# Sliding-window attention with a gated SwiGLU: edge blocks in smaller TensorE tiles, V for sixteen heads at a time

## Chip, cores and metric

The kernel runs on one core of one Trainium2 chip. The metric is the device time of one launch in microseconds (us). Three runs are timed, and a further execution is profiled.

## What is computed

```python
def reference(A_x, A_wqkv, A_wo, B_x, B_w1, B_w3, B_w2, gate_w):
    ...
        H = 32; Dh = D // H; W = 256
        qkv = (lambda x, *d: x.transpose(*d))((x @ wqkv).reshape(B, S, 3, H, Dh), 2, 0, 3, 1, 4)
        q, k, v = qkv[0], qkv[1], qkv[2]
        scores = jnp.einsum("bhqd,bhkd->bhqk", q, k) * (Dh ** -0.5)
        idx = jnp.arange(S)
        mask = (idx[:, None] - idx[None, :] >= 0) & (idx[:, None] - idx[None, :] < W)
        scores = jnp.where(mask[None, None], scores, -1e9)
        p = _softmax(scores, axis=-1)
        o = jnp.einsum("bhqk,bhkd->bhqd", p, v)
        return (lambda x, *d: x.transpose(*d))(o, 0, 2, 1, 3).reshape(B, S, D) @ wo
    ...
        gate = jnp.einsum("bsd,df->bsf", x, w1)
        up = jnp.einsum("bsd,df->bsf", x, w3)
        h = _silu(gate) * up
        out = jnp.einsum("bsf,fd->bsd", h, w2)
    ...
    g = _sigmoid((x * gate_w).sum(-1, keepdims=True))
    a = _A_ref(x, A_wqkv, A_wo)
    b = _B_ref(x, B_w1, B_w3, B_w2)
    return g * a + (1 - g) * b
```

B = 1, S = 2048, D = 512, F = 1376, all in bfloat16; both branches read A_x.

## The kernel before

**Attention.** The 32 heads of 16 channels go in four groups c of eight heads; a group's 128 channels fill the partitions, two heads (a = 0, 1) in each strip s of 32. `projections(c, tq)` computes K, Q and V for 512 tokens (L422 for K and Q, L499 for V). Since a strip holds two heads, K is kept once for each head with the other head's channels zeroed: `kz` and `k1`, made by masks at L465 and a copy at L462 (for c = 0 at L443, L448 and L453). `kz` has four blocks of 64 keys for each 128-key block t, so that two neighbouring ones hold the same 64 keys of both heads.

Keys come in 16 blocks t of 128. For queries P*t+64 to P*t+320 the whole block is scored: `main_batch(c, t)` makes eight products of 32 rows x 128 weight columns over 256 queries into the PSUM tile `su` (L560), ScalarE takes the exponential into `Em` (L564), and GpSimd cuts the two triangles (L569, L574). The 64 queries before (low) and after (high) see half the block: `edge_batch(c, h)` puts those of four blocks into one `su` (L610): 64 queries against a 128-column weight tile that holds 64 keys of both heads. After the exponential (L614) GpSimd cuts the low triangles (L627, two selects) and VectorE the high ones (L633, for the last batch L637 too, with the masks `medge` and `mlast`). The last key block's own 64 queries ride in the last edge batch.

`pv(c, w)` makes the value products for 512 queries (L700): for each head a of a strip one PSUM bank `ch`, four strips at once (128 rows x 17 columns, the 17th gives the softmax's sum). Mains and edges are mixed, first all of a = 0, then all of a = 1. The edges' values lie in two further parts of `vs` (LO, HI), in which the rows of the other head's keys are zero; L271 and L272 clear them, and GpSimd copies the halves (L517) after VectorE has evicted V (L512). Two 32x32-block transposes (L724), a reciprocal, a multiplication and a transpose back (L734) make the normalized output `OT`.

**The rest.** The SwiGLU runs beside it: w1 and w3 products into `ch` (L825), tanh on ScalarE (L835), two multiplications on VectorE (L839, L845), the w2 products (L875) and an eviction scaled by 1 - g (L880). 32 of the last 96 columns of F go another way, `tail_columns` (L785). The gate g comes as a 129th column of V's products in the first group (`wv0`, L521). `output` multiplies by wo (L905), adds, and stores.

**What sets the order.** A planner (`Plan.emit`) simulates the engines and buffers ahead of time and writes one fixed order for each engine. Every operation has a duration, dependencies, a due time (from the dictionary K) and the buffers it takes and frees: one `su`, four `ch` banks (shared by projections, V, value products, SwiGLU and output), nine `Em`, two `Ee`. For TensorE it knows forms: "full", "row" (scores) and "column" (value products), charges 0.117 us for a change, and `rank` moves due times so that operations of small forms stand together: earlier by `beside` when a small form is loaded, later by `apart` for "column" when "full" is.

Of the kernel before, what the change touches and what calls it, by code (L numbers as in the profile page):

```python
# [7 lines left out]
ALU = mybir.AluOpType  # L8
# [37 lines left out]
class Plan:  # L46
# [101 lines left out]
def kernel(  # L148
# [27 lines left out]
    NV = NT * 4  # L176
    LO, HI = NV, 2 * NV
    VW = DH + 1
    HALF = (0, 1, 2, 3, 4)
    SCALE = float(DH) ** -0.5  # L180
# [17 lines left out]
    wB = pp.tile([P, NDC, 2 * FB], BF16, name="wB")  # L198
# [8 lines left out]
    wv0 = pp.tile([P, NDC, P + 4], BF16, name="wv0")  # L207
# [8 lines left out]
    mlast = pp.tile([P, 2, KB], BF16, name="mlast")  # L216
    Em = [pp.tile([P, 4, 2, 256], BF16, name=f"Em_{i}") for i in range(9)]
    Ee = [pp.tile([P, 4, 4, 2, KB], BF16, name=f"Ee_{i}") for i in range(2)]
    kt = [pp.tile([P, 512], BF16, name=f"kt_{i}") for i in range(2)]
# [10 lines left out]
    K = {"T0": 6.663, "TA": 234.789, "TF0": -1.359, "TF1": 251.583, "PV": 0.213, "EDGE": -2.966, "HOLD": -4.301, "LEAD": 9.863, "QLEAD": -3.864, "V": 5.26, "O0": -0.819, "O1": 5.827, "O2": 6.852, "O3": 24.592, "FE": -3.084, "PE": -2.787, "VE": -3.291, "MK": 4.4, "UP": 2.598, "_km": 1.0, "_lo": 1.0, "LE": 4.467, "ADJ": 0.265, "SEP": 1.114, "BE": -2.825}  # L230
    plan = Plan({"su": 1, "ch": 4, "Em": len(Em), "Ee": len(Ee), "kt": 2, "tt": 2, "h1": 2,
# [4 lines left out]

    def half_of(base, a):
        return slice(0, KB) if (a == 1) == (base == LO) else slice(KB, P)
# [19 lines left out]
    def constants3():  # L258
        nc.gpsimd.memset(qT[:, S:S + KB], 0.0)
        for m in (medge, mlast):  # L260
            nc.gpsimd.memset(m[:], BIG)
        for m, k, sign, halves in ((medge, 0, 1, (0, KB)), (medge, 1, -1, (0, KB)),
                                   (mlast, 0, 1, (0, KB)), (mlast, 1, 1, (KB,))):
            for lo in halves:
                nc.gpsimd.affine_select(out=m[lo:lo + KB, k, :], in_=m[lo:lo + KB, k, :],
                                        pattern=[[sign, KB]], compare_op=ALU.is_ge, fill=0.0,
                                        base=0 if sign > 0 else -1, channel_multiplier=-sign)

    def constants4():
        nc.gpsimd.memset(hb[:], 0.0)  # L270
        nc.vector.memset(vs[:, LO:LO + NV, :], 0.0)  # L271
        nc.vector.memset(vs[:, HI:HI + NV, :], 0.0)  # L272
        nc.gpsimd.memset(vs[:, 0:NV, DH:2 * VW:VW], 1.0)
        for base in (LO, HI):
            for a in range(2):
                nc.gpsimd.memset(vs[half_of(base, a), base:base + NV, a * VW + DH], 1.0)

# [106 lines left out]
    def gw_out():  # L384
        nc.vector.tensor_copy(out=wv0[:, :, P:P + 1],
                              in_=ch[gjob.at["ch"]][:].bitcast(BF16)[:, 0:NDC].rearrange("p (c o) -> p c o", o=1))

    def wv0_copy():
        nc.vector.tensor_copy(out=wv0[:, :, 0:P], in_=wqkv_sb[:, :, 2 * D:2 * D + P])

    a = add("PE", 0.1, gw_turn, [gw_in], 9.407, take=[(gjob, "ch")])
    wv0_ready = [add("DVE", 0.15, gw_out, [a], 9.0, free=[(gjob, "ch")]),
                 add("DVE", 0.3, wv0_copy, [qkv_in[2]], 9.0)]
# [11 lines left out]
    def projections(c, tq):  # L405
# [3 lines left out]
        if c:  # L409
            war = [su_ops[(c - 1, t)] for t in range(4 * tq, 4 * tq + 4)]  # L410
            war.append(far_ops[(c - 1, tq)])
            vwar = [pv_ops[(c - 1, w)] for w in range(tq, min(NTC, tq + 2))]
            qwar = [su_ops[(c - 1, t)] for t in range(max(0, 4 * tq - 3), 4 * tq + 4)]
            qwar += [far_ops[(c - 1, h)] for h in range(max(0, tq - 1), tq + 1)]
        else:
            vwar, qwar = [], []
# [16 lines left out]
        kv0 = kz[:, 4 * tq:4 * tq + 4, 1:3, :]  # L433
        kv1 = kz[:, 4 * tq:4 * tq + 4, 0:4:3, :]

        k1v = k1[:, 4 * tq:4 * tq + 4, :, :]

        def by_half(src):
            return src.rearrange("p (k h t) -> p k h t", h=2, t=KB)
        a = project(kj, D, [qkv_in[0 if c < 2 else 3]], due, [(kj, "ch")])  # L440
        if c == 0:
            def kev_a():
                nc.vector.tensor_scalar_mul(  # L443
                    out=kv0, in0=by_half(ch[kj.at["ch"]][:]),
                    scalar1=rowsA[:, 0:1])

            def kev_b():
                nc.scalar.activation(  # L448
                    out=k1v, in_=by_half(ch[kj.at["ch"]][:]),
                    func=ACT.Copy, scale=rowsA[:, 1:2])  # L450
            b = add("DVE", 0.69, kev_a, [a], due, free=[(kj, "ch")])
            def kev_c():
                nc.gpsimd.tensor_copy(out=kv1, in_=k1v)  # L453
            m = add("ACT", 0.69, kev_b, [b], due, free=[(kj, "ch")])
            k_ready[(c, tq)] = [b, m]
            ke_ready[(c, tq)] = [add("POOL", 0.62, kev_c, [m], due)]
        else:
            def kev():
                nc.vector.tensor_copy(out=kt[kj.at["kt"]][:], in_=ch[kj.at["ch"]][:])

            def kcopy():
                (nc.vector if K["_km"] else nc.gpsimd).tensor_copy(out=kv1, in_=k1v)  # L462

            def kmask(h):
                (nc.vector if K["_km"] else nc.gpsimd).tensor_scalar_mul(  # L465
                    out=(kv0, kv1, k1v)[h], in0=by_half(kt[kj.at["kt"]][:]),
                    scalar1=rowsA[:, min(h, 1):min(h, 1) + 1])
            b = add("DVE", 0.69, kev, [a], due, take=[(kj, "kt")], free=[(kj, "ch")])
            k_ready[(c, tq)] = [add("DVE" if K["_km"] else "POOL", 0.3 if K["_km"] else 1.64, lambda h=h: kmask(h), [b] + war, due, free=[(kj, "kt")])
                                for h in (0, 2)]  # L470
            ke_ready[(c, tq)] = [add("DVE" if K["_km"] else "POOL", 0.3 if K["_km"] else 0.62, kcopy, k_ready[(c, tq)], due)]
# [12 lines left out]

        vdue = due + K["V"]
        res = []
        gates = []
        for m0, nm in ([(4 * tq, 2), (4 * tq + 2, 2)] if c == 0 else [(4 * tq, 4)]):
            vj = Job()
            w = P + 1 if c == 0 else P  # L490

            def vmm(lo, hi, vj=vj, m0=m0, w=w):
                pst = ch[vj.at["ch"]]
                for mm in range(lo, hi):
                    m = m0 + mm
                    for dc in range(NDC):
                        rhs = (wv0[:, dc, 0:w] if c == 0
                               else wqkv_sb[:, dc, 2 * D + c * P:2 * D + (c + 1) * P])
                        nc.tensor.matmul(pst[:, mm * w:(mm + 1) * w], lhsT=xT[:, dc, m * P:(m + 1) * P],  # L499
                                         rhs=rhs, start=(dc == 0), stop=(dc == NDC - 1))  # L500

            def v_of(rows, base, a, m0=m0, nm=nm):
                return vs[rows, base + 4 * m0:base + 4 * (m0 + nm), a * VW:a * VW + DH]

            def v_all(vj=vj, m0=m0, nm=nm, w=w):
# [463 lines left out]
```

## Time and profile before

| | |
|---|---|
| median of three timed runs | 240.3 us (240.14 to 240.38) |
| the profiled execution's own time | 240.56 us |
| its span in the profile | 238.8 us |
| granted TensorE clock | 1.00 |
| VectorE busy | 201.3 us (84%) |
| TensorE's waits for others, longest line | 1.7 us, two times (L700 for L839) |

The page lists for each engine its busy time in the span. PE is TensorE's matmuls and PEld its weight loads, which lie beside them; DVE is VectorE, ACT ScalarE, POOL GpSimd. Groups of instructions are named by line, engine, operation and tiles. In the timeline the first two columns are the start and the length of a run of equal instructions in us; matmuls overlap, so that a group's length is not the time that it takes from the next one: that is seen from start to start. A bracket at the end gives idle time of the engine before the instruction and what ended it.

### The profile page before, as it was taken

What the parts mean: (1) busy time and instruction counts of PE and PEld (TensorE: products, weight loads), DVE (VectorE), ACT (ScalarE), POOL (GpSimd) and SP (SyncE); (2) the same over time, 40 slices, a digit from 0 to 9 for tenths busy, and PEclk for the clock granted to TensorE, in tenths of its full rate; (3) what the DMA queues carried; (4) which work ended last, traced back from release to release, by engine and by line L of the source; (5) the groups of instructions that cost most, each with busy time, mean ns of one, the idle gap of its engine ahead of it and who ended that gap; (6) DMA issues with size and microseconds to landing.
All of it is one profiled execution on the core that took longest, in us unless ns stands there. A gap on an engine that the chain in (4) does not pass through costs nothing.

```text
span 238.8 us, 8528 instructions
## 1 busy us (share of the span) xinstructions
PE 231.3 (97%) x3738; PEld 118.8 (50%) x3738; DVE 201.3 (84%) x342; ACT 171.2 (72%) x141; POOL 159.6 (67%) x261
## 2 busy tenths in 40 slices
PE   8999999999999999999989899999999999999994
PEld 8554544546463543545454544545454545445442
DVE  5576998967699989996699999987899897969885
ACT  3389798876867898666858788776768989766510
POOL 7259967979857877587475777768494968575500
PEclk9999999999999999999999999999999999999999
DMA  7999980000000000000000000000000001002133
GB/s 199 205 335 276 201 212 17 5 1 3 3 3 0 5 11 11 7 0 3 3 3 3 1 8 20 3 0 3 3 3 5 3 0 25 3 22 69 52 108 110
DMA packets 20413, 11.59 MB, mean 49 GB/s; under 512 B 9656, under 2 KB 20376, under 8 KB 20376
## 3 DMA queue, kind: packets, MB, share of 16 engines
q1 hardware_dynamic: 19680, 10.59, 17.7%
q8 instruction: 29, 0.48, 0.9%
q10 hardware_dynamic: 696, 0.46, 0.6%
q14 instruction: 8, 0.07, 0.1%
HBM read 6.85 MB, written 2.10 MB: 37 GB/s over the span
## 4 chain that ended last, share of the span: by engine, by line
PE 72%; DVE 19%; ACT 4%; issue 2%; POOL 1%; DVEq 0%; ACTq 0%
PE ch L825 20%; PE ch L875 15%; PE ch L422 9%; PE ch L700 8%; PE su L560 6%; PE ch L905 5%; PE ch L499 4%; ACT Ee L614 4%; DVE h L839 3%; PE su L610 2%; DVE Ee L633 2%; DVE hT L845 2%; DVE Ee L637 2%; DVE tn L724 2%; DVE k L465 2%
## 5 line engine op out<-in xcount | busy, mean ns | idle before, releaser
L564 ACT ACTIVATE Em<-su 128x2048 bf16<-128x2048 f32 x60 | 112.6, 1877 | 34.6 <-PE su L560 31.4
L825 PE MATMUL ch<-xT,w_sb 128*128 128x512 bf16 x320 | 79.3, 380 | 0.5 <-DVE vs L512 0.3
L569 POOL TENSOR_SCALAR_AFFINE_SELECT Em<-Em 64x512 bf16<-64x512 bf16 x60 | 41.1, 685 | 32.5 <-ACT Em L564 26.9
L627 POOL TENSOR_SCALAR_AFFINE_SELECT Ee<-Ee 64x1024 bf16<-64x1024 bf16 x32 | 42.7, 1333 | 21.4 <-ACT Ee L614 19.3
L825 PEld LDWEIGHTS <-w_sb 128*128 128x128 bf16 x320 | 28.4, 98 | 34.8 <-issue 6.9
L875 PE MATMUL ch<-w_sb,hT 128*128 128x512 bf16 x160 | 40.3, 380 | 0.0
L574 POOL TENSOR_SCALAR_AFFINE_SELECT Em<-Em 64x512 bf16<-64x512 bf16 x56 | 37.3, 665 | 3.2
L614 ACT ACTIVATE Ee<-su 128x2048 bf16<-128x2048 f32 x16 | 30.0, 1876 | 10.3 <-PE su L610 7.6
L422 PE MATMUL ch<-xT,wqkv_sb 128*128 128x512 bf16 (+1 forms) x136 | 34.3, 372 | 0.0
L517 POOL COPY vs<-vs 64x256 bf16<-64x256 bf16 (+1 forms) x80 | 30.6, 382 | 5.1 <-DVE vs L512 1.8
L839 DVE SCALAR_TENSOR_TENSOR h<-tt,ch 128x512 bf16<-128x512 bf16 (+1 forms) x44 | 29.6, 677 | 4.7 <-ACT tt L835 4.5
L845 DVE SCALAR_TENSOR_TENSOR hT<-h,ch 128x512 bf16<-128x512 bf16 x40 | 27.1, 677 | 1.9
L835 ACT ACTIVATE tt<-ch 128x512 bf16<-128x512 f32 (+1 forms) x44 | 25.7, 594 | 2.4 <-PE ch L825 2.2
L700 PEld LDWEIGHTS <-vs 128*17 128x17 bf16 x1664 | 21.1, 92 | 8.6 <-issue 6.3
L700 PE MATMUL ch<-Em,vs 128*17 128x256 bf16 (+2 forms) x672 | 22.9, 242 | 2.4 <-DVE h L839 1.7
L700 PE MATMUL ch<-Ee,vs 128*17 128x64 bf16 x992 | 22.6, 193 | 0.0
L875 PEld LDWEIGHTS <-hT 128*128 128x128 bf16 x160 | 13.9, 98 | 16.8 <-issue 3.2
L422 PEld LDWEIGHTS <-wqkv_sb 128*128 128x128 bf16 x136 | 12.4, 99 | 12.7 <-issue 2.1
L499 PEld LDWEIGHTS <-xT 128*128 128x128 bf16 x256 | 15.8, 97 | 5.6 <-issue 1.8
L880 DVE TENSOR_SCALAR bsb<-ch,omg 128x512 bf16<-128x512 f32 x15 | 11.2, 747 | 7.6 <-PE ch L875 7.4
L560 PE MATMUL su<-qT,kz 32*128 32x256 bf16 x240 | 17.3, 278 | 0.2
L560 PE MATMUL su<-qT,k 32*128 32x256 bf16 x240 | 16.7, 268 | 0.0
(81 smaller groups left out, 257.4 us busy)
## 6 DMA issues: line engine op xcount, KB each, us to landing
out_dram<-ot SPq DMA_DIRECT2D x15, 128.0 KB, 1.7
wqkv_sb<-in_A_wqkv_dram SPq DMA_DIRECT2D x5, 256.0 KB, 5.7
w_sb<-in_B_w_dram SPq DMA_DIRECT2D x1, 1280.0 KB, 6.7
w_sb<-in_B_w_dram SPq DMA_DIRECT2D x2, 608.0 KB, 7.8
w_sb<-in_B_w_dram SPq DMA_DIRECT2D x2, 512.0 KB, 5.2
w_sb<-in_B_w_dram SPq DMA_DIRECT2D x2, 256.0 KB, 4.9
wo_sb<-in_A_wo_dram SPq DMA_DIRECT2D x1, 512.0 KB, 5.5
xs<-in_A_x_dram SPq DMA_DIRECT2D x1, 256.0 KB, 2.9
```

Of the source, the lines that this page charges most:

```text
L422: nc.tensor.matmul(pst[:, t0:t1], lhsT=wqkv_sb[:, dc, col + c * P:col + (c + 1) * P], rhs=xT[:, dc, tq * 512 + t0:tq * 512 + t1], start=(d ...
L560: nc.tensor.matmul(su[:, s, a * 256:(a + 1) * 256], lhsT=head_keys(r, t, a), rhs=qT[r, q0:q0 + 256], start=True, stop=True)
L564: nc.scalar.activation(out=Em[job.at["Em"]][:], in_=su[:].rearrange("p s (a q) -> p s a q", a=2), func=ACT.Exp, scale=SCALE)
L569: nc.gpsimd.affine_select(out=e, in_=e, pattern=[[0, 8], [1, KB]], compare_op=ALU.is_ge, fill=0.0, base=0, channel_multiplier=-1)
L574: nc.gpsimd.affine_select(out=e, in_=e, pattern=[[0, 8], [-1, KB]], compare_op=ALU.is_ge, fill=0.0, base=-1, channel_multiplier=1)
L614: nc.scalar.activation(out=Ee[ej.at["Ee"]][:].rearrange("p s t k q -> p s (t k q)"), in_=su[:], func=ACT.Exp, scale=SCALE)
L627: nc.gpsimd.affine_select(out=e, in_=e, pattern=[[0, 4], [0, 4], [1, KB]], compare_op=ALU.is_ge, fill=0.0, base=0, channel_multiplier=-1)
L700: nc.tensor.matmul(po[32 * s:32 * s + VW, lo - 512 * w:hi - 512 * w], lhsT=vs[:, i, a * VW:(a + 1) * VW], rhs=mov, start=(n == 0), stop=(n ...
L825: nc.tensor.matmul(ch[job.at["ch"]][:], lhsT=wA[:, dc, :] if joint else w[:, dc, f * P:(f + 1) * P], rhs=xT[:, dc, tcb * 512:(tcb + 1) * 512],
L839: nc.vector.scalar_tensor_tensor(out=h1[job.at["h1"]][ru, :], in0=tt[job.at["tt"]][rg, :], scalar=1.0, in1=ch[job.at["ch"]][rg, :], op0=AL ...
L845: nc.vector.scalar_tensor_tensor(out=dst, in0=h1[job.at["h1"]][ru, :], scalar=0.5, in1=ch[up.at["ch"]][ru, :], op0=ALU.mult, op1=ALU.mult)
L875: nc.tensor.matmul(bps[:], lhsT=ht[:, mm * P:(mm + 1) * P], rhs=w2_sb[0:fs, f, :], start=(f == 0), stop=(f == NFC - 1))
```

## The change

Edge scores become products of 32 rows x 64 weight columns, one for each head (a in either half of the output partitions). Edge probabilities then hold head 0's keys in partitions 0 to 63 and head 1's in 64 to 127, and edge values become products of 64 rows x 17 columns, both heads' at once; this is a form of its own, "half", and comes after the mains of both heads. K is two plain tables `kh`. V is made for two groups at once, 256 columns, when c is even. `vs` has no zeroed parts; where a head's keys lie in the other half of the partitions, GpSimd copies their values into `vx`. With `_lo` = 0 the low triangles are cut by VectorE (`cut(0)`), not by GpSimd. The last key block's own queries ride in the main batch of the block before it, with one more GpSimd select. The gate is a 65th column of the tail products. `kt` is replaced by the output buffers `ot`. All due times in K are new (`SEP` becomes `apart`, `ADJ` `beside`).

```diff
@@ -72,7 +72,7 @@
-            elif op.form == "column":
+            elif op.form != "row":
                 due += self.apart
...
-    kz = pp.tile([P, NT, 4, KB], BF16, name="kz")
-    qT = pp.tile([P, S + KB], BF16, name="qT")
-    k1 = pp.tile([P, NT, 2, KB], BF16, name="k1")
-    vs = pp.tile([P, 3 * NV, 2 * VW], BF16, name="vs")
+    kh = pp.tile([P, 2, S], BF16, name="kh")
+    qT = pp.tile([P, S], BF16, name="qT")
+    vs = pp.tile([P, 2, NT, 16, VW], BF16, name="vs")
+    vx = pp.tile([P, NT, 8, VW], BF16, name="vx")
...
-    K = {"T0": 6.663, "TA": 234.789, "TF0": -1.359, "TF1": 251.583, "PV": 0.213, "EDGE": -2.966, "HOLD": -4.301, "LEAD": 9.863, "QLEAD": -3.864, "V": 5.26, "O0": -0.819, "O1": 5.827, "O2": 6.852, "O3": 24.592, "FE": -3.084, "PE": -2.787, "VE": -3.291, "MK": 4.4, "UP": 2.598, "_km": 1.0, "_lo": 1.0, "LE": 4.467, "ADJ": 0.265, "SEP": 1.114, "BE": -2.825}
+    K = {"T0": 4.901, "TA": 240.002, "TF0": -0.302, "TF1": 259.743, "PV": -2.143, "EDGE": -3.049, "HOLD": -0.789, "LEAD": 6.264, "QLEAD": -3.642, "V": 6.712, "O0": -0.237, "O1": 3.776, "O2": 9.951, "O3": 19.933, "FE": -0.555, "PE": -3.535, "VE": -9.063, "MK": 2.536, "UP": 1.059, "_km": 1.0, "_lo": 0.0, "LE": 3.346, "ADJ": 0.254, "SEP": 3.156, "BE": -3.008}
...
-        nc.vector.memset(vs[:, LO:LO + NV, :], 0.0)
-        nc.vector.memset(vs[:, HI:HI + NV, :], 0.0)
...
+        nc.gpsimd.memset(vs[:, :, :, :, DH:VW], 1.0)
+        nc.gpsimd.memset(vx[:, :, :, DH:VW], 1.0)
...
             def kmask(h):
+                keng.tensor_scalar_mul(out=kv[h], in0=ot[kj.at["ot"]][:], scalar1=rowsA[:, h:h + 1])
...
+        if c % 2:
+            return
         vdue = due + K["V"]
...
+        for m0 in (4 * tq, 4 * tq + 2):
...
+                        nc.tensor.matmul(pst[:, mm * 256:(mm + 1) * 256], lhsT=xT[:, dc, m * P:(m + 1) * P],
+                                         rhs=wqkv_sb[:, dc, 2 * D + cp * 256:2 * D + cp * 256 + 256],
+                                         start=(dc == 0), stop=(dc == NDC - 1))
...
+            def vcross(a, m0=m0):
+                to, at_ = slice(KB * a, KB * a + KB), slice(KB - KB * a, P - KB * a)
+                nc.gpsimd.tensor_copy(out=vx[to, m0:m0 + 2, :, 0:DH], in_=vs[at_, cp, m0:m0 + 2, a:16:2, 0:DH])
...
+                    n = min(256, S - q0)
+                    nc.tensor.matmul(su[:, s, a * 256:a * 256 + n], lhsT=kh[r, a, P * t:P * t + P],
+                                     rhs=qT[r, q0:q0 + n], start=True, stop=True)
+                    if t == NT - 2:
+                        nc.tensor.matmul(su[:, s, a * 256 + n:(a + 1) * 256], lhsT=kh[r, a, P * t + P:P * t + 2 * P],
+                                         rhs=qT[r, S - KB:S], start=True, stop=True)
...
+                    k0, q0 = P * t + KB * k, P * t + 320 * k
+                    for a in range(2):
+                        for s in range(4):
+                            r = slice(32 * s, 32 * s + 32)
+                            if q0 < S:
+                                nc.tensor.matmul(su[KB * a:KB * a + KB, s, (2 * i + k) * KB:(2 * i + k + 1) * KB],
+                                                 lhsT=kh[r, a, k0:k0 + KB], rhs=qT[r, q0:q0 + KB],
+                                                 start=True, stop=True)
...
+        def cut(k):
+            e = Ee[ej.at["Ee"]][:, :, 0:4 if k == 0 or h < NTC - 1 else 2, k, :]
+            nc.vector.tensor_tensor(out=e, in0=e, in1=medge[:, k][:, None, None, :].to_broadcast([P, 4, e.shape[2], KB]),
                                     op=ALU.min)
...
+            edge_ready[(c, h)] = [add("DVE", 1.09, lambda: cut(0), [x], due - K["MK"])]
+        edge_ready[(c, h)].append(add("DVE", 1.09, lambda: cut(1), [x], due - K["MK"]))
...
+        def edges(last):
+            for n, (t, q, k) in enumerate(lows + highs):
+                for a in range(2):
+                    rows = slice(KB * a, KB * a + KB)
+                    for s in range(4):
+                        values = (vs[rows, c // 2, t, 8 * (c % 2) + 2 * s + a, :] if a == k
+                                  else vx[rows, t, 4 * (c % 2) + s, :])
+                        product(a, s, values, Ee[ejob[(c, "e", t // 4)].at["Ee"]][rows, s, t % 4, k, :], q - q0,
+                                last and n == len(lows + highs) - 1)
...
         for a in range(2):
-            prev = add("PE", streams(0, cut), lambda a=a: mm(a, 0, cut), deps + [prev], due, take=[(jobs[a], "ch")], free=frees,
-                       form="column")
-            ends.append(prev)
+            prev = add("PE", streams(early), lambda a=a: mains(a, early), mdeps + [prev], due, take=[(jobs[a], "ch")],
+                       free=mfree, form="column")
+        prev = add("PE", 0.25, lambda: edges(not final), edeps + [prev], due,
+                   free=[(ejob[(c, "e", h)], "Ee") for h in range(max(0, w - 1), w + 1)], form="half")
+        ends = [prev, prev]
         if final:
             for a in range(2):
-                prev = ends[a] = add("PE", 0.1, lambda a=a: mm(a, cut, cut + 1), [prev] + main_ready[(c, NT - 2)], due,
-                                     free=frees, form="column")
+                prev = ends[a] = add("PE", 0.12, lambda a=a: mains(a, [NT - 2, NT - 1], True),
+                                     [prev] + main_ready[(c, NT - 2)], due, free=[(ejob[(c, NT - 2)], "Em")],
+                                     form="column")
...
-            a = add("PE", 0.47, mm_b, list(xt_ready[tcb]) + w_ab, due, take=[(job, "ch")])
+            a = add("PE", 0.49, mm_b, list(xt_ready[tcb]) + w_ab + [gw_ready], due, take=[(job, "ch")])
+            z = add("ACT", 0.19, zact, [a], due, free=[(job, "ch")])
+            gate_ready.append(add("DVE", 0.3, zg, [z], due))
```

More of the change, by code (lines that the diff above doesn't have):

```diff
@@ L461, in kcopy @@
-            def kcopy():
-                (nc.vector if K["_km"] else nc.gpsimd).tensor_copy(out=kv1, in_=k1v)
+                nc.vector.tensor_copy(out=ot[kj.at["ot"]][:], in_=ch[kj.at["ch"]][:])
             def kmask(h):
[L465 to L468, printed above, removed]
@@ L473, in projections @@
+            k_ready[(c, tq)] = [add("DVE" if K["_km"] else "POOL", 0.3 if K["_km"] else 1.64, lambda h=h: kmask(h),
+                                    [b] + war, due, free=[(kj, "ot")]) for h in range(2)]
         qj = Job()
@@ L680, in pv @@
-        frees += [(ejob[(c, "e", h)], "Ee") for h in range(max(0, w - 1), w + 1)]
+        q0 = 512 * w
+        tiles = list(range(max(0, 4 * w - 2), 4 * w + 4))
+        lows = [(t, P * t, 0) for t in tiles if t >= 4 * w]
+        highs = [(t, P * t + 320, 1) for t in tiles if t < 4 * w + 2 and P * t + 320 < S]
+        vdeps = sum((v_ready[(c // 2, h)] for h in range(max(0, w - 1), w + 1)), [])
+        edeps = vdeps + sum((edge_ready[(c, h)] for h in range(max(0, w - 1), w + 1)), [])
         rj = Job()
@@ L704, in streams, with product @@
-        def streams(n0, n1):
-            return 0.035 + sum(hi - lo for kind, t, lo, hi in todo[n0:n1]) / 2400
-        cut = len(todo) - 1 if final else len(todo)
-        ends = []
+        begun = set()
+        def product(a, s, values, e, col, last):
+            first = (a, s) not in begun
+            begun.add((a, s))
+            nc.tensor.matmul(ch[jobs[a].at["ch"]][32 * s:32 * s + VW, col:col + e.shape[-1]], lhsT=values, rhs=e,
+                             start=first, stop=last, skip_group_check=True)
```

245 lines of the change are left out of this document (62 added, 183 removed).

## The prediction

> **What bounds the kernel now.** I read the page's busy shares first, then the chain that ended last, then TensorE's own waits.
>
> ```profile
> PE 231.3 (97%) x3738; PEld 118.8 (50%) x3738; DVE 201.3 (84%) x342; ACT 171.2 (72%) x141; POOL 159.6 (67%) x261
> PE 72%; DVE 19%; ACT 4%; issue 2%; POOL 1%; DVEq 0%; ACTq 0%
> ```
>
> TensorE (PE) is the bound in every stage: in the stretches of 40 us it is busy 38.2 to 39.9 us each, and the granted clock is 1.00 in all of them. VectorE (DVE) is next, with 38.8 of 40 us busy from 120 to 160 us. So the question is how many ns TensorE's queue needs after the change, and whether VectorE still empties the PSUM banks in time. "Busy" hides that matmuls overlap, so I go by the distance from one start to the next, in the timeline:
>
> ```profile
> 108.44 0.38 PE L875 MATMUL ch<-w_sb,hT 128*128 128x512 bf16 x1
> 108.75 0.21 PE L700 MATMUL ch<-Em,vs 128*17 128x64 bf16 x4
> ...
> 109.40 0.20 PE L700 MATMUL ch<-Ee,vs 128*17 128x64 bf16 x4
> 109.43 0.20 PE L700 MATMUL ch<-Em,vs 128*17 128x64 bf16 x4
> 109.46 0.20 PE L700 MATMUL ch<-Ee,vs 128*17 128x64 bf16 x4
> ...
> 110.08 0.20 PE L700 MATMUL ch<-Ee,vs 128*17 128x64 bf16 x4
> 110.21 0.29 PE L560 MATMUL su<-qT,kz 32*128 32x256 bf16 x4
> ```
>
> Two prices stand here. Four 64-column products, one for each strip of 32 output partitions, follow each other every 0.03 us (108.75 to 110.08 gives 28 ns for a step of 64 columns): the four run at once and the stream of columns sets the pace. And each change of tile shape costs extra: a 512-column product takes 216 ns in a run of its kind (1.73 us for eight of L875 in the chain), but 0.31 us pass before L700 starts, and 0.13 instead of 0.03 us pass from L700 to L560. So one change of shape costs about 95 ns.
>
> ```profile
> 102.00 0.41 PE L610 MATMUL su<-qT,kz 32*128 32x64 bf16 x32
> 102.35 1.04 PE L422 MATMUL ch<-xT,wqkv_sb 128*128 128x512 bf16 x4
> ```
>
> The 32 edge scores of a batch take 0.35 us: 95 ns for the change back and about 0.25 us, or eight steps of some 29 to 31 ns, for the work.
>
> TensorE's waits are few, and they have one origin worth knowing:
>
> ```profile
> PE ch L700 <- DVE h L839: 1.7, 2, 0.9
> PE ch L700 <- DVE hT L845: 0.5, 1, 0.5
> ```
>
> ```profile
> 118.12 2.69 POOL L627 TENSOR_SCALAR_AFFINE_SELECT Ee<-Ee 64x1024 bf16<-64x1024 bf16 x2 [2.05 <-ACT Ee L614]
> 118.43 1.36 DVE L637 TENSOR_TENSOR Ee<-Ee,mlast 128x512 bf16<-128x512 bf16 x1
> 119.72 1.24 DVE L462 COPY kz<-k 128x512 bf16<-128x512 bf16 x1
> 120.88 0.67 DVE L839 SCALAR_TENSOR_TENSOR h<-tt,ch 128x512 bf16<-128x512 bf16 x1
> 121.60 0.21 PE L700 MATMUL ch<-Em,vs 128*17 128x64 bf16 x4 [0.89 <-DVE h L839]
> ```
>
> Beside the two long selects of GpSimd (POOL, L627), VectorE's SBUF-to-SBUF operations end when GpSimd's do: L462 takes 1.24 us here and 0.28 us elsewhere, L637 1.36 us always. Then L839, which frees a PSUM bank, is late, and TensorE waits 0.89 us. The stall at 134.9 us (0.76 us) has the same ancestry (L633 1.16, L465 1.24 beside L627).
>
> **The change, part by part, on TensorE.**
>
> Edge value products. Of the 992 small products of L700 with Ee, 32 belong to the last key block and stay what they are; 960 become 64x32 tiles. Now they make 240 steps of four at 28 ns, 6.7 us. If eight run at once, 120 steps remain. No row shows eight at once; the nearest (L610, L700) show four starting about 4 ns apart, so eight starts fill 29 to 32 ns. At 30 ns that is 3.6 us: **3.1 us saved**, between 0 (they do not overlap) and 3.4.
>
> Change of shape. Mains keep 128x32 tiles, edges get their own shape and come after both heads' mains. A pair of banks passes from 3 changes (in, to L560, out) to 4, in 16 places, and the last one, which returns to mains, adds one more: 17 x 95 ns = **1.6 us added**. More if the planner puts other work between mains and edges; two more changes for each such place.
>
> Edge scores. 512 products in 128 steps of 29 ns become 960 in 120 steps of 30 ns, each with 64 weight columns rather than 128: 3.7 against 3.6 us, **nothing**, if the eight overlap; twice the steps (+3.2 us) if only four do. What a 64-column load costs in this shape is not in the trace. From below: L785 repeats a 64-column product with a full 128-column load (0.47 us for sixteen), so a full load fits into 29 ns. From above: if the two loads for one strip of rows go one after the other at that rate, a step takes 58 ns. I take the first, since L610's loads hide completely today.
>
> Column tiling, says the Trainium skill in "TensorEngine Tiling (Array Packing)", section "Restrictions", disables the fast weight load; "TensorE: Matmul & The Clock Gate", section "LDWEIGHTS (loading the stationary operand)", gives columns/1.2 ns for a load. As an estimate by that page, 64 columns take 53 ns, a step of the edge scores would be bound by its load, and the sum would be 120 x 23 ns = 2.8 us higher, 240.9 us in the end. No row here shows a 64-column load, so the trace neither agrees nor differs; the rival on weight loads below has the same effect, priced from rows.
>
> V for sixteen heads. 256 products of 128 columns at 56 ns (0.89 us for sixteen, L499 in the chain) become 128 of 256 columns at 109 ns (512 columns take 216, so 0.42 ns a column): 14.4 to 14.0 us, **0.5 us saved**. The 65th column of L785 is worth 0.03 us. Block 14's scores are split into 192 and 64 columns: same columns, nothing. V's work for the second and fourth head groups moves ahead into the first and third; TensorE has the same total, and its load is the first 256 V columns, which the opening fetches already.
>
> TensorE sum: -3.1 + 1.6 + 0 - 0.5 = **-2.0 us**.
>
> **The other engines.** VectorE loses L462 (4.8), the two masks at L465 (14.7), L637 (5.4), the memsets L271 and L272 (1.9) and L389 (0.3): 27.1 us. It gains 24 contiguous masks (0.34 us alone, 0.61 at today's mean: 8 to 15) and the lower cut of 16 edge batches that GpSimd had (0.69 to 0.98 each: 11 to 16). V's evictions are 16 x 0.69 against 11.9. So VectorE lands between 8 us less and 4 more, most likely some 4 less, and does not become the bound. GpSimd loses L627 (42.7), L517 (30.6) and L453 (2.4) and gains 32 copies at 0.43, four selects at 0.68 and a few us of ones: near 100 us. ScalarE keeps its 76 exponentials. The gate's activation moves from V to the tail columns, always before the eviction that needs it: nothing.
>
> So GpSimd no longer holds VectorE for 1.3 us at a time. The stalls above (0.89 + 0.76 us) and the one at 94 us (0.5 us, after L633 of 1.53 us beside L627) are 2.2 us; the new cut on VectorE is itself work ahead of L839, so I count half back: -1.1. Against it: both heads' banks are now held until the edges are done. The second bank is wanted about 0.22 us sooner (half of the 1.33 us from 108.75 to 110.08, against 0.45 us for one head's 1,024 columns of mains), and the first turn (L724, 0.70 us) starts only behind the edges. 16 x 0.22 = 3.5 us at most; today 4 of the 16 entries wait for a bank, so a quarter: +0.9.
>
> The order itself is redone, since all due times in the dictionary K change. Waits of TensorE in the waits view come to 4.2 us, so order alone can give no more than that, and I take it at nothing.
>
> Sum: -2.0 - 1.1 + 0.9 = -2.2 us. The profiled execution took 240.56 us (span 238.8), 0.26 above the median of 240.3; taken from the median, **238.1 us**.
>
> **Rivals.**
> *Banks are the new wait (slower).* If each of the 16 value stages waits the whole 0.22 us, and no stall goes because the new cuts delay L839 as the selects did: -2.0 + 3.5 = +1.5, 241.8 us. It decides from 0.13 us a stage on, where it has used up the 2.0. For: VectorE at 97% from 120 to 160 us, and all of today's L700 waits are for banks. Against: 12 of 16 entries do not wait.
> *Weight loads bind the edge scores (slower).* Two loads in a row for each strip: 120 steps x 58 instead of 30 ns adds 3.4 us, 241.5 us. For: twice the loads in each step. Against: loads hide behind matmuls in every row seen.
> *Eight tiles do not overlap.* No edge saving, edge scores doubled: +1.6 - 0.5 + 3.2 = +4.3, less 0.2 of waits: 244.4 us. The change would then not do what it says.
> *The saving is eaten.* No stall goes and half the bank price is paid: -2.0 + 1.8, 240.1 us.
>
> **How the numbers follow.** Forecast 0.57; eaten 0.10; loads 0.13; banks 0.15; no overlap 0.05. A measurement here tells 0.2% (0.5 us) from no change. Only the forecast is faster: 0.57; the eaten one and an edge of the loads are within: 0.11; the rest slower: 0.32. Low end: 3.4 saved on the edges, all 2.2 of stalls gone and no bank price: -4.5, so 235.8 us. High end, with loads and banks inside: 242.2 us; no overlap and the tails stay out.
>
> **What would show it.** Edge products: eight starts, then the next eight 29 to 32 ns on, and each edge block 0.25 us; 53 or more is the loads. Changes of shape: 95 ns at mains to edges, with nothing between. Stalls: no VectorE SBUF operation over about 1 us, and TensorE's waits in all under 4 us; waits at the mains' second bank would be the bank rival. VectorE near 197 us. I am wrong if TensorE's start-to-start total does not fall by 1.5 us or more, or if it falls and the waits grow by as much.

## The result, and the profile after

The changed kernel takes 242.87 us (median of four, 242.26 to 243.06) against 240.22 us: a ratio of 1.0109, with a 95% interval of 1.0090 to 1.0128. It is slower; 238.1 us was forecast, and the range ended at 242.2. The profiled execution took 242.26 us (span 240.6), 1.70 more than that of before. Line numbers from here on are the changed kernel's: L586 is now the value products, L542 the edge scores, L490 and L493 the main scores, L747 and L797 w1/w3 and w2, L459 V.

The page's busy shares and the chain:

```profile
PE 235.0 (98%) x4090; PEld 119.4 (50%) x4090; DVE 189.1 (79%) x327; ACT 171.6 (71%) x137; POOL 105.0 (44%) x173
PE 92%; DVE 3%; DMA 2%; issue 1%; ACT 1%; DVEq 0%; ACTq 0%
```

VectorE has 12 us less work, GpSimd 55 less, and nearly the whole chain is TensorE's. TensorE's waits for others, all of them:

```profile
PE su L281 <- DVE warm L284: 1.1, 1, 1.1
PE ch L747 <- DVE h L761: 0.6, 1, 0.6
PE ch L366 <- DMA gwr<-in_gate_w_dram: 0.2, 1, 0.2
```

1.9 us in place of 4.2. So the time is lost in TensorE's own work. Counted from the first start of a block of products to the first start of the next block, all such blocks of a kind added up (us; the last block of output has no next one and is left out):

| block | before | after | |
|---|---|---|---|
| edge scores | 5.51 | 9.78 | +4.27 |
| value stages | 22.77 | 24.23 | +1.46 |
| tail columns | 1.87 | 2.31 | +0.44 |
| main scores | 19.78 | 19.84 | +0.06 |
| V | 17.32 | 14.81 | -2.51 |
| w1/w3 | 78.42 | 76.87 | -1.55 |
| opening transposes | 1.71 | 0.97 | -0.74 |
| K and Q, w2, output | 80.41 | 80.27 | -0.14 |

The sum is +1.29. The first start is at 1.06 us in both kernels; what follows the last product, evictions and stores, takes 3.63 us instead of 3.19. Together that is the 1.7 us by which the span grew. A wait is counted with the block before it. So 1.65 of the 2.51 us that V lost are the two waits of 0.89 and 0.76 us for L839, which stood behind blocks of V; of the 4.1 us that V and w1/w3 lost, only 0.5 were forecast from V's columns.

The timeline of the kernel after, at a batch of edge scores and at the edge values of one stage:

```profile
46.29 1.24 PE L797 MATMUL ch<-w_sb,hT 128*128 128x512 bf16 x5
47.46 0.71 PE L542 MATMUL su<-qT,kh 32*64 32x64 bf16 x64
48.10 0.82 PE L402 MATMUL ch<-xT,wqkv_sb 128*128 128x512 bf16 x3
...
54.72 1.06 PE L586 MATMUL ch<-Em,vs 128*17 128x64 bf16 x48
55.71 0.20 PE L586 MATMUL ch<-Ee,vs 64*17 64x64 bf16 x4
55.72 0.20 PE L586 MATMUL ch<-Ee,vx 64*17 64x64 bf16 x4
55.74 0.20 PE L586 MATMUL ch<-Ee,vs 64*17 64x64 bf16 x4
...
55.80 0.20 PE L586 MATMUL ch<-Ee,vs 64*17 64x64 bf16 x4
55.81 0.33 PE L586 MATMUL ch<-Ee,vx 64*17 64x64 bf16 x8
55.96 0.22 PE L586 MATMUL ch<-Ee,vs 64*17 64x64 bf16 x4
56.00 0.22 PE L586 MATMUL ch<-Ee,vx 64*17 64x64 bf16 x4
56.03 0.22 PE L586 MATMUL ch<-Ee,vs 64*17 64x64 bf16 x4
...
56.16 0.22 PE L586 MATMUL ch<-Ee,vs 64*17 64x64 bf16 x4
56.31 0.40 PE L490 MATMUL su<-qT,kh 32*128 32x256 bf16 x8
```

The 64 scores of a batch take 0.64 us to the next block where 0.35 were expected (0.25 and a change of shape). The values show how: up to 55.81 each four follow after 0.015 us, so eight tiles do run at once, 30 ns for eight, as forecast. Then comes a hole, and from 55.96 on each four take 0.033 us, **8.3 ns a product**. In the starts of single products of both lines it is the same: the first 32 stand 3.7 to 4.5 ns apart on average, then one hole of about 100 ns, then 8.3 ns each to the end. In one batch of scores, the 16th, 32nd, 48th and 64th product start 76, 139, 363 and 497 ns after the first; in the values 56, 117, 347 and 480.

My theory from this: TensorE is supplied with load and product pairs at 8.3 ns each, and what collects during a change of shape (some 32 pairs) hides it at first. Before the change no run of small products was long enough to show it: 32 scores in a batch, and in the value stages products of 192 and 256 columns in between. The rivals: the loads of 64 columns, the stream of columns through a tile, and the order or waits.

### The profile page after: what moved, and what is told of

Its sections match the earlier page's. It is cut to its first block, busy times and chain, and to the rows that moved or that the text cites. A ratio compares the mean times of both kernels' runs of the same rounds, so it can differ in the third digit from the quotient of the medians.

```text
span 240.6 us, 9112 instructions
## 1 busy us (share of the span) xinstructions
PE 235.0 (98%) x4090; PEld 119.4 (50%) x4090; DVE 189.1 (79%) x327; ACT 171.6 (71%) x137; POOL 105.0 (44%) x173
## 4 chain that ended last, share of the span: by engine, by line
PE 92%; DVE 3%; DMA 2%; issue 1%; ACT 1%; DVEq 0%; ACTq 0%
PE ch L747 29%; PE ch L797 16%; PE ch L402 12%; PE ch L586 9%; PE su L490 8%; PE ch L459 6%; PE ch L827 6%; PE su L542 4%; DMA gwr<-in_gate_w_dram 2%; PE ch L695 1%; DVE h L761 1%; DVE tn L634 1%; DVE nt L640 0%; DVE kh L430 0%; DVE OT L644 0%
## 5 line engine op out<-in xcount | busy, mean ns | idle before, releaser
L502 POOL TENSOR_SCALAR_AFFINE_SELECT Em<-Em 64x512 bf16<-64x512 bf16 x64 | 44.1, 693 | 106.0 <-ACT Em L497 104.5
L747 PE MATMUL ch<-xT,w_sb 128*128 128x512 bf16 x320 | 78.9, 380 | 0.6 <-DVE h L761 0.6
L747 PEld LDWEIGHTS <-w_sb 128*128 128x128 bf16 x320 | 28.9, 98 | 35.8 <-issue 6.4
L507 POOL TENSOR_SCALAR_AFFINE_SELECT Em<-Em 64x512 bf16<-64x512 bf16 x56 | 39.4, 703 | 3.4
L797 PE MATMUL ch<-w_sb,hT 128*128 128x512 bf16 x160 | 39.7, 380 | 0.0
L586 PEld LDWEIGHTS <-vs 128*17 128x17 bf16 (+1 forms) x1184 | 19.7, 88 | 9.8 <-issue 6.4
L557 DVE TENSOR_TENSOR Ee<-Ee,medge 128x1024 bf16<-128x1024 bf16 (+1 forms) x32 | 20.4, 679 | 4.5 <-ACT Ee L547 4.3
L490 PE MATMUL su<-qT,kh 32*128 32x256 bf16 (+1 forms) x480 | 23.8, 271 | 0.0
L797 PEld LDWEIGHTS <-hT 128*128 128x128 bf16 x160 | 14.5, 98 | 17.7 <-issue 1.9
L472 POOL COPY vx<-vs 64x256 bf16<-64x256 bf16 x32 | 14.7, 461 | 7.6 <-DVE vs L464 6.4
L459 PE MATMUL ch<-wqkv_sb,xT 128*128 128x256 bf16 x128 | 16.7, 273 | 0.0
L490 PEld LDWEIGHTS <-kh 32*128 32x128 bf16 x480 | 7.6, 92 | 17.7 <-issue 16.5
L586 PE MATMUL ch<-Em,vs 128*17 128x192 bf16 (+2 forms) x704 | 16.3, 239 | 0.0
L634 DVE STREAM_TRANSPOSE xs<-ch 128x512 f32<-128x512 f32 x16 | 10.5, 696 | 7.3 <-PE ch L586 7.3
```

The lines of the kernel that those rows point to most:

```text
L459: nc.tensor.matmul(pst[:, mm * 256:(mm + 1) * 256], lhsT=xT[:, dc, m * P:(m + 1) * P], rhs=wqkv_sb[:, dc, 2 * D + cp * 256:2 * D + cp * 25 ...
L490: nc.tensor.matmul(su[:, s, a * 256:a * 256 + n], lhsT=kh[r, a, P * t:P * t + P], rhs=qT[r, q0:q0 + n], start=True, stop=True)
L502: nc.gpsimd.affine_select(out=e, in_=e, pattern=[[0, 8], [1, KB]], compare_op=ALU.is_ge, fill=0.0, base=0, channel_multiplier=-1)
L507: nc.gpsimd.affine_select(out=e, in_=e, pattern=[[0, 8], [-1, KB]], compare_op=ALU.is_ge, fill=0.0, base=-1, channel_multiplier=1)
L586: nc.tensor.matmul(ch[jobs[a].at["ch"]][32 * s:32 * s + VW, col:col + e.shape[-1]], lhsT=values, rhs=e, start=first, stop=last, skip_group ...
L747: nc.tensor.matmul(ch[job.at["ch"]][:], lhsT=wA[:, dc, :] if joint else w[:, dc, f * P:(f + 1) * P], rhs=xT[:, dc, tcb * 512:(tcb + 1) * 512],
```

## The experiments

Kernels of a group ran on one chip, each compared with the kernel before there (239.99, 240.34, 240.00, 240.04 us for the four groups). Where "one execution" stands, the kernel was timed once.

**Is it the number of pairs?** e1 takes the edge scores back to 32 pairs of 128 weight columns, with everything else as changed. e2 leaves out half of the edge scores of each batch. e3 streams only 32 of the 64 queries through the edge values (the other half is not computed).

```diff
# e1
-    kh = pp.tile([P, 2, S], BF16, name="kh")
+    kz = pp.tile([P, NT, 6, KB], BF16, name="kz")
...
+                            nc.tensor.matmul(su[:, s, (2 * i + k) * KB:(2 * i + k + 1) * KB],
+                                             lhsT=kz[r, t, 4 * k:4 * k + 2, :].rearrange("p b x -> p (b x)"),
+                                             rhs=qT[r, q0:q0 + KB], start=True, stop=True)
# e2, in the edge scores
-                for i in range(4):
+                for i in range(2):
# e3, the edge values' moving operand
-  Ee[...][rows, s, t % 4, k, :]
+  Ee[...][rows, s, t % 4, k, 0:KB // 2]
```

> The changed kernel with the edge scores alone as before: 32 products of 32 rows x 128 weight columns a batch, two heads in one, from a key table with six blocks of 64 (two small copies more for each projection), and one buffer less for the exponentials (8) to make room. Edge values, V and the cuts stay as changed. Supply theory (TensorE is fed one load and product per 8.3 ns once some 32 queued pairs are used up, so the number of small products counts, not their size): the edge scores' line falls from 9.8 to about 5.5 us, 238.5 us in all. Weight-load theory (the 64-column loads are slow): the same here. Tile theory (eight tiles do not run at once): the same here. If instead the loss lies in the new order or in waits: no gain, 242.5 us or more, because VectorE gets 24 more copies.

> The changed kernel with only the first 32 of 64 (or 48) edge score products of each batch; the other two blocks' edge scores are left out. Supply theory: all 32 start 3.5 to 4.5 ns apart, 0.14 us and no hole; the line falls from 9.8 to about 3.8 us, some 236.7 us in all. Weight-load or tile theory: half of the products, half of the time, so the line falls to about 5.6 us, 238.6 us in all.

> The changed kernel with edge value products over 32 instead of 64 queries each; half of the queries' edge values are left out, the number of products is the same. Supply theory: nothing moves, still 8.3 ns a product after the first 32, line total of the 64-row products 9.1 us, 242.5 us in all. Tile theory (the stream of columns through tiles that do not overlap sets the 8.3 ns): products at 4 to 5 ns, the line near 6 us, 239.5 us in all. Weight-load theory: nothing moves, as with supply.

e1: 239.63 us, ratio 0.9987 (0.9977 to 0.9996); its score line takes 5.28 us, 4.5 less than in the kernel after, as expected. The time falls by 3.2 only, 1.1 short of what was expected: there are two more copies for each projection, 8 in all on GpSimd and 24 on VectorE (192.7 us busy in place of 189.1), and the w1/w3 blocks take 1.45 us more. e2: 237.54 us (one execution), between its two outcomes, and the line 4.20, nearer to the 3.8 of the supply theory than to 5.6. The timeline of e2, where a batch is now 32 pairs:

```profile
47.46 0.33 PE L542 MATMUL su<-qT,kh 32*64 32x64 bf16 x32
47.72 1.04 PE L402 MATMUL ch<-xT,wqkv_sb 128*128 128x512 bf16 x4
```

32 pairs take 0.26 us to the next block, change included; 64 took 0.64. Half the pairs cost 40%: there is no hole and no slow part. These 32 pairs have the same 64-column loads, which start within 0.11 us, and the products within 0.14 us, so a 64-column load does not in itself take 8.3 ns of TensorE's time. e3: 242.92 us (one execution). Its timeline:

```profile
56.73 0.18 PE L586 MATMUL ch<-Ee,vs 64*17 64x32 bf16 x4
56.74 0.31 PE L586 MATMUL ch<-Ee,vx 64*17 64x32 bf16 x8
56.88 0.20 PE L586 MATMUL ch<-Ee,vs 64*17 64x32 bf16 x4
56.92 0.20 PE L586 MATMUL ch<-Ee,vx 64*17 64x32 bf16 x4
56.95 0.20 PE L586 MATMUL ch<-Ee,vs 64*17 64x32 bf16 x4
```

Half the columns, and the steps of four are still 0.033 us: the stream through a tile isn't it. (Whether the loads are it, e3 cannot tell: it leaves them as they are. But L586 loads 17 weight columns and L542 64, and both end at the same 8.3 ns, so the width of the load isn't it either.)

**Does it belong to the new shapes?** e9 is the kernel before with its edge values grouped behind both heads' mains and only 32 of 64 queries streamed, in the old 128x17 shape.

```diff
# e9
+        todo.sort(key=lambda x: x[0] != "main")
...
-                        mov = e[:, t % 4, k, :]
+                        hi = lo + KB // 2
+                        mov = e[:, t % 4, k, 0:KB // 2]
...
+                fn = lambda: (mm(1, 0, wide), mm(0, wide, cut), mm(1, wide, cut))
```

> The kernel before with its edge value products, still 128 rows x 17 columns and four at a time, over 32 instead of 64 queries, and both heads' edge products together at the end of each value stage; half of the queries' edge values are left out. The stream would allow 3.4 ns a product. Supply theory: some 32 start about 3.5 ns apart, then a hole of some 100 ns, then 8.3 ns a product, in this shape as in the changed kernel's two; the 64 take about 0.48 us, and the time stays near 240.3 us. Tile theory (only the shapes with 64 rows or 64 columns are slow): 3.5 to 4 ns for all 64, 0.24 us, about 237 us in all.

241.79 us (one execution), 1.5 above what was expected: not a gain, with half the columns. The starts decide here. Its timeline:

```profile
55.74 1.06 PE L703 MATMUL ch<-Em,vs 128*17 128x64 bf16 x48
56.62 0.72 PE L703 MATMUL ch<-Ee,vs 128*17 128x32 bf16 x64
57.27 0.29 PE L560 MATMUL su<-qT,kz 32*128 32x256 bf16 x4
```

64 products take 0.65 us with the change, 10 ns each all in all. Of the single starts, about the first 24 come in steps of 25 ns for four, then each is 8.3 ns behind the one before: 1050, 1058, 1067, 1075, 1083 ns. There is no hole of 100 ns (the longest step is 35), and the quick part is slower than the new shapes', but the 8.3 ns is the old shape's too.

**Can wide products refill the queue?** e4 puts two wide products (256 columns, both in the same tile, overwritten later) into the middle of each batch of edge scores.

```diff
# e4, inside the edge scores at i == 2
+   for _ in range(2):
+       nc.tensor.matmul(su[0:KB, 0, 256:512], lhsT=kh[0:32, 0, P * t:P * t + KB],
+                        rhs=qT[0:32, P * t:P * t + 256], start=True, stop=True)
```

> The changed kernel with two more products of 256 columns, of the same tile shape (32 rows x 64 weight columns), in the middle of each edge score batch; their result is overwritten. They add 16 x 0.21 = 3.4 us of stream. Supply theory: the queue fills while they run, the hole of about 100 ns is hidden and 13 to 25 of the products behind them start 3.5 to 4.5 ns apart, so a batch takes 0.5 to 0.6 us as now and the time stays within 0.8 us of the changed kernel's. Weight-load or tile theory: the second half still goes at 8.3 ns and the batch grows by the whole 0.21 us, 245.5 us or more in all.

```profile
34.71 0.33 PE L546 MATMUL su<-qT,kh 32*64 32x64 bf16 x32
34.95 0.26 PE L538 MATMUL su<-qT,kh 32*64 32x256 bf16 x1
34.97 0.28 PE L546 MATMUL su<-qT,kh 32*64 32x64 bf16 x9
35.06 0.27 PE L538 MATMUL su<-qT,kh 32*64 32x256 bf16 x1
35.06 0.48 PE L546 MATMUL su<-qT,kh 32*64 32x64 bf16 x23
```

245.46 us (one execution): missed. In the timeline the wide products take one tile, one after the other, and the small ones go on beside them in the others, most of them 8 to 17 ns apart, so nothing was held back that could have collected. The experiment did not create what it was to test; whether waiting refills the store stays open.

**Both shapes back, with the rest of the change.** e6 has e1's scores and edge values as 128-row products against a zero-padded table again; V for sixteen heads, the cuts on VectorE, the gate's place and all due times stay. e7 and e8 exchange one number: the low cuts' engine.

```diff
# e6, besides e1's scores
+    vz = pp.tile([P, 2, NT, 8, VW], BF16, name="vz")
...
+                    product(a, s, vz[:, k, t, 2 * s + a, :], Ee[...][:, s, t % 4, k, :], q - q0,
+                            last and n == len(lows + highs) - 1)
# e7, in the kernel after
-  "_lo": 0.0
+  "_lo": 1.0
# e8, in the kernel before
-  "_lo": 1.0
+  "_lo": 0.0
```

> The changed kernel with edge scores and edge values both in the old shapes: 32 products of 128 weight columns a batch from the six-block key table, and values as 128x17 products from tables whose other rows are zero, in the mains' form and behind each head's mains; V for sixteen heads, the gate in the tail columns and the cuts on VectorE stay. Nine buffers for exponentials again. Supply theory: beside e1_pairs (239.6 us) the two forms of the value products (15.1 + 9.1 us to the next block) become one of about 22.8 us, since a 64-column product of four at a time needs 7 ns, under the 8.3 that the supply gives, and 13 to 17 changes of shape go: 238.1 us. If the rest of the loss is order or waits, and not the small products: 239.5 us or more, with GpSimd's 32 copies more.

> The changed kernel with the low triangles cut by GpSimd's long selects again (two for each edge batch) and not by VectorE; all else as changed. If the long selects held VectorE and so the banks: VectorE's SBUF operations over 1 us come back, TensorE's waits rise from under 1 to about 3 us, 245.3 us. If the waits went because of the new order or the fewer copies: within 0.6 us of the changed kernel, 242.9 us.

> The kernel before with its own switch for the low triangles turned: VectorE cuts both triangles of an edge batch in four operations, GpSimd's two long selects go; nothing else moves but the order that the planner derives from it. If the long selects caused the waits: TensorE's waits fall from 4.2 to about 2 us, 238.2 us. If not: VectorE, some 5 to 10 us busier, makes it 240.2 to 241.5 us.

e6: 242.83 us, 1.0108 (1.0083 to 1.0134): missed by far. e8: 242.10, 1.0087 (1.0053 to 1.0122), above both of its outcomes. e7: 244.63, 1.0182 (1.0156 to 1.0209), between its two, nearer to 245.3. TensorE's longest line of waits in e6:

```profile
PE su L504 <- ACT Em L511: 5.6, 7, 1.5
```

The same in e8:

```profile
PE su L560 <- ACT Em L564: 3.6, 4, 1.4
```

And in e7:

```profile
PE ch L459 <- DVE h L761: 1.4, 2, 1.0
```

In e6 and e8 TensorE waits for score tiles that ScalarE has not yet emptied, a wait that neither of the two kernels has. The due times in K had been set for other pieces: the planner's own forecast is 240.7 for e6 against 233.0 for the kernel after. An edit that keeps the due times is not a clean undo here, and e6 says nothing on the shapes yet.

**The same with due times of their own.** For each set of pieces new values of K were searched by the planner's own forecast, so that all are ordered about equally well: e10 and e10b are e6, e11 is e8, e12 is e7, e13 and e13b are the kernel before, e14 the kernel after. e15 is the kernel after with two costs in the planner corrected to what the trace shows.

```diff
# e15, besides K
-  add("PE", 0.25, lambda: edges(not final), ...
+  add("PE", 0.48, lambda: edges(not final), ...
# and the edge scores' mm
-  add("PE", 0.232, mm, ...
+  add("PE", 0.51, mm, ...
```

> e6_both with other due times in K and nothing else: e6_both waited 5.6 us for ScalarE and the exponentials' buffers, in an order that its due times made for other pieces, and the planner's own forecast for it is 240.7, against 233.0 for the changed kernel; the due times here bring the forecast to 233.1. Supply theory, with the order repaired: e1_pairs (239.6 us) less 1.5 us of value products and their changes of shape, 238.0 us, below both kernels. If the old value shape in itself is no better than the new: 239.6 us or more.

> The same with a second, independent set of due times (the planner's forecast 233.3). Supply theory: 238.0 us, within 0.7 us of the other set. If the set of due times decides more than the shapes do: the two differ by over 1 us.

> e8_before_lo0 (the kernel before, all low triangles cut by VectorE) with other due times: e8 itself waited 3.6 us for ScalarE, and the planner forecast 239.7 against 233.3 for the kernel before; here it is 233.6. If GpSimd's long selects caused the kernel before's waits for banks: no VectorE operation over 1 us, waits for VectorE under 1.5 us, 238.4 us. If not: 240 us or more.

> e7_lo (the changed kernel with GpSimd's long selects for the low triangles) with other due times: the planner's forecast falls from 234.2 to 232.3, below the changed kernel's 233.0, so that order no longer speaks against it. If the long selects hold VectorE: 244 us or more still, and VectorE operations over 1 us. If e7_lo was slower for its order: 242 us or less.

> The kernel before with nothing changed but its due times in K, found from those of e11_before_cuts and with GpSimd's long selects kept (planner's forecast 233.4, its own due times 233.3). If the selects caused the waits that e11_before_cuts (238.2 us) lost: VectorE operations over 1 us stay, and 239.5 us or more. If it was the order alone: 238.5 us or less.

> The same with a second set of due times (forecast 233.2). Selects: 239.5 us or more. Order: 238.5 us or less.

> The changed kernel with nothing changed but its due times (planner's forecast 232.5 instead of 233.0). Supply theory: the 1,920 small products cost what they cost, 241.8 to 243.3 us. If the changed kernel's loss lies in its order: under 241 us.

> The changed kernel with the planner told what the small products take (0.51 us for a batch of edge scores instead of 0.232, 0.48 us for the edge values instead of 0.25) and due times found with these costs. Supply theory: at most the waits of under 1 us can go, 242 to 243.5 us. If the planner's wrong costs made an order that loses the time: 241 us or less.

| kernel | edge shapes | low cuts | us | ratio (95%) |
|---|---|---|---|---|
| e13, e13b | old | GpSimd | 238.87, 239.21 | 0.9940 (0.9910 to 0.9970), 0.9957 (0.9933 to 0.9981) |
| e11 | old | VectorE | 238.21 | 0.9922 (0.9906 to 0.9939) |
| e10, e10b (rest of the change in) | old | VectorE | 236.31, 236.07 | 0.9843 (0.9828 to 0.9859), 0.9837 (0.9818 to 0.9856) |
| e14, e15 | new | VectorE | 241.80, 241.97 | 1.0067 (1.0044 to 1.0090), 1.0081 (1.0050 to 1.0113) |
| e12 | new | GpSimd | 242.52 | 1.0102 (1.0082 to 1.0121) |

The new shapes, with the tables that they need, cost 5.5 to 5.9 us (e14, e15 against e10, e10b; the groups ran on two chips, and by the ratios it is 5.4 to 5.9). e10 and e10b came out 1.7 and 1.9 us below the 238.0 expected; why stays open. With its costs told truly the planner finds nothing better: in e14 and e15 the score line still takes 9.74 and 9.69 us, the edge values 9.14 and 9.17. Order alone is worth about 1 us to either kernel. With the cuts on VectorE the kernel before came out 0.7 to 1.0 us faster (e11 against e13, e13b), but the intervals overlap, e13 and e13b ended between the two outcomes named for them, and a gain is not shown. V for sixteen heads with all that is left of the change brings 1.9 to 2.1 (e10, e10b against e11; not separated further). e10b, at 236.07 us, beats both kernels. The busy shares of e10b:

```profile
PE 225.0 (96%) x3576; PEld 115.9 (50%) x3610; DVE 194.8 (83%) x353; ACT 170.9 (73%) x137; POOL 122.0 (52%) x216
```

TensorE is busy 10 us less than in the kernel after; the record lacks 34 of its 3,610 products, so a part of that is not real (the span is 6.4 us shorter). The timeline of a value stage in e10b:

```profile
57.05 0.62 PE L602 MATMUL ch<-Em,vs 128*17 128x64 bf16 x24
57.50 0.42 PE L602 MATMUL ch<-Ee,vz 128*17 128x64 bf16 x32
57.73 0.63 PE L602 MATMUL ch<-Em,vs 128*17 128x64 bf16 x24
58.17 0.42 PE L602 MATMUL ch<-Ee,vz 128*17 128x64 bf16 x32
58.53 0.40 PE L504 MATMUL su<-qT,kz 32*128 32x256 bf16 x8
```

Here a head's 32 edge products in four tiles take 0.23 us (57.50 to 57.73), 7.2 ns each, and no change of shape stands ahead of them. Two heads take 0.46 us: about what the 64 products of eight tiles take (0.48 from first to last start), which have a change of shape ahead of them besides.

e12 was to show whether the long selects of GpSimd cost TensorE 2 us. At 242.52 it came out between its outcomes (244 or more, 242 or less) and does not show it. Two of its groups (busy and mean after the first bar):

```profile
L552 POOL TENSOR_SCALAR_AFFINE_SELECT Ee<-Ee 64x1024 bf16<-64x1024 bf16 x32 | 42.6, 1330 | 20.8 <-ACT Ee L547 16.2 <-PE ch L797 1.8 <-PE ch L747 1.7
L557 DVE TENSOR_TENSOR Ee<-Ee,medge 128x1024 bf16<-128x1024 bf16 (+1 forms) x16 | 15.0, 936 | 4.4 <-ACT Ee L547 4.2
```

TensorE's waits for VectorE in e12, the opening's left out:

```profile
PE ch L459 <- DVE h L761: 0.4, 1, 0.4
...
PE ch L747 <- DVE h L761: 0.3, 1, 0.3
```

The selects are back and lengthen VectorE's masks (mean 936 ns; 679 in the kernel after), but under this order TensorE waits 0.7 us for VectorE in all.

## Why the prediction was wrong, step by step

- **Edge values: the step that failed.** "At 30 ns that is 3.6 us: 3.1 us saved" took the pace of four starts, 4 ns apart, for a pace that lasts. The trace has it, for 32 products. Without their change of shape the edge values of a stage (60 on average) last 0.475 us, 7.6 us in all, 4.0 more than forecast and 0.9 more than the 6.7 of before. The stages as a whole rose by 1.46 where -1.5 was forecast, since their mains took about 1 us less than I had left them; why stays open.
- **Edge scores: the same step.** "Nothing" turned out as +4.27 us. The batch of before has 32 pairs, just what runs at the quick pace, so the row that I took the price from (0.25 us for 32) could not show the other one. Both ends of my bounds (nothing, +3.2 to 3.4 us) lay below it.
- **The two together** are 7.2 us off: -1.5 forecast, +5.7 measured. The experiments agree: 5.5 to 5.9 us at like order.
- **Changes of shape were right.** 172 became 189, the 17 forecast, at about 95 ns each; in 4 of 16 stages other work stands between mains and edges.
- **The rival "eight tiles do not overlap"** came nearest for the edge work (0 + 1.6 + 3.2 = +4.8 us, against +5.7) and for the wrong reason: they overlap, and what comes behind the first 32 pairs does not keep up. **Weight loads**, as a rival priced by the load of one strip after another, fall: in e2 eight 64-column loads pass with their products in 32 ns, not 58 (the 9th, 17th and 25th product start 52, 84 and 116 ns after the first). The Trainium skill's columns/1.2 ns for a load ("TensorE: Matmul & The Clock Gate", section "LDWEIGHTS (loading the stationary operand)") gave +2.8 us, the right sign and 1.5 short of the +4.27, for a reason that the runs refute: 17 weight columns and 64 give the same 8.3 ns. The same page's Part 3, section "The mechanism", speaks of a 64-deep reorder window; if loads and products both count, the 32 pairs seen in the new shapes would fit that number. No run here shows that it is the window, and the quick part of e9 had 24.
- **Banks** did not become the wait: no line of them is left at the value products, and the +0.9 counted for them was not paid.
- **Waits and V.** -0.5 for V and -0.2 for waits were forecast; all that is not edge work came to -4.0 us. The direction was right, the size missed by 3.3, which hid nearly half of the 7.2. That was luck for the number. About 2 of the 3.3 can be named: TensorE's waits fell from 4.2 to 1.9 us, by 2.3, where -0.2 was forecast, since the stalls went whole and not by half and no bank price came in their place. Order was to give nothing; e13 shows that it alone takes 0.8 to 1.2 us off the kernel before. That leaves 1.70 measured against -2.2: 3.9 off.
- **Long operations on VectorE.** Those over 1 us fell from 14 (18.3 us) to 2 (2.15 us), nearly as forecast. The masks show it (one line's instructions; min/median/max in ns). In the kernel after:

```profile
L557 DVE TENSOR_TENSOR Ee<-Ee,medge x32: 417/686/886, 22.2 to 220.0; 128x1024 bf16<-128x1024 bf16 x28, 128x512 bf16<-128x512 bf16 x4
```

In the kernel before:

```profile
L633 DVE TENSOR_TENSOR Ee<-Ee,medge x16: 425/693/1630, 22.8 to 223.0; 128x1024 bf16<-128x1024 bf16 x12, 128x512 bf16<-128x512 bf16 x4
```

The longest mask falls from 1,630 to 886 ns. The Trainium skill ("SBUF — State Buffer", section "SBUF: two separate sides") has it that GpSimd and a VectorE operation with two SBUF inputs shut each other out; the trace agrees: in the kernel before, a mask of 128x1024 that starts while a long select runs takes up to 1,630 ns, and 693 where the mask is there first and the select takes 1.67 us in place of 1.15. VectorE's total is 189 us where I said 197. That TensorE gains by it at like order is not shown: the cuts alone came out at 0.7 to 1.0 us (e11 against e13, e13b), with intervals that overlap.

**Open:** that pairs collect while TensorE changes shape is argued from the starts, not shown; what the hole of some 100 ns is; whether 8.3 ns belongs to a pair or half of it to each instruction, since loads and products were never tried apart; what the two us of e10 over e11 consist of.

## What to carry to other kernels

When products become smaller and more, price them by their number as well as their columns: here the old profile showed starts 4 ns apart in rows of at most 32 equal products, and 64 in a row cost 8.3 ns each from the 33rd on, after a hole of 100. Giving the edge values tiles of half the rows, eight instead of four, gained nothing, at 0.48 us for 64 products against 0.46, and the extra change of shape and the doubled number of scores were pure cost. Where a planner sets the order, search it anew for each variant, or the comparison measures the due times (e6 and e10 have the same pieces and differ by 6.5 us).

## What the runs showed that I had not expected

The supply of small products: in 32x64 and 64x32 tiles 3.5 to 4.5 ns apart on average for about 32, a hole of 85 to 108 ns, then 8.3 ns. In 128x32 tiles (e9) about 24 at 6 to 7 ns, no such hole, then the same 8.3 ns. It came out the same with 17 or 64 weight columns and 32 or 64 moving ones. And a product of 256 columns in one tile does not hold up small ones that go to other tiles (e4): beside it most kept their 8.3 ns, some steps were 15 to 17.
